# Attention and a capacity-routed mixture of experts on one core: high parts of late w2 pieces ahead of the plane copies, one expert's last roundings 6 matmuls sooner, and a small product kept in PSUM

## The chip, the cores and the metric

The kernel runs on one core of one Trainium2 chip. The metric is device time in microseconds (us), lower is better. The time before is a median of 895.79 us over 3 runs (895.22 to 896.08).

The core's engines run side by side, each through its own list of instructions in order, and they wait for one another by semaphores: TensorE (PE in the profile; PEld is its weight load), VectorE (DVE), ScalarE (ACT), GpSimd (POOL) and SyncE (SP). SBUF is the on-chip working memory; PSUM is the memory that matmuls write and that the other engines, GpSimd excepted, read.

## The reference

Two stages. Attention on 8 x 12 heads, 448 rows of 64, with scores capped by a tanh, gives x of 3584 tokens x 768 features. Then each token goes to exactly one of 8 experts, each of which takes at most 448 tokens, in the order of all (token, expert) logits:

```python
logits = x @ w_gate                       # 3584 x 8
for idx in np.argsort(-logits.flatten()):
    tok, e = idx // E, idx % E
    if assigned[tok] >= 0 or counts[e] >= cap: continue
    assigned[tok] = e; counts[e] += 1
for e in range(E):
    h = np.maximum(x[mask_e] @ w1[e], 0.0)   # 448x768 @ 768x1024
    out[mask_e] = h @ w2[e]                  # 448x1024 @ 1024x768
```

All of it is float32.

## The kernel before

**Three stages.** Attention comes first (to about 330 us of the span). A first choice follows, and from about 381 us to the end the experts run one after the other. Experts are called 0 to 7 here, in the order in which they run; the "third expert" is expert 2. This case is about experts 2 to 6.

**An expert.** Its two products are 144 and 176 matmuls. A float32 operand is split into a high part, rounded to the matmul's faster float32 format, and a low part that is the difference, and a product is the sum high x high, high x low, low x high. In `ffn1` (line 869) eight column blocks of w1 (pieces 0 to 7) are multiplied into the gathered tokens. In `ffn2` (line 900) the work is eight units: units 0 to 3 are the four token tiles with the first half of the output columns (pieces 0 to 3 of w2), units 4 to 7 the same tiles with the second half (pieces 4 to 7). In unit 4 the 16 matmuls with high parts come first, then the 8 with low parts, two for each of pieces 4, 5, 6, 7.

**Splitting weights.** `cut` (lines 757 to 765) makes the two parts of a piece: ScalarE writes the high part (line 760, `w1h` or `w2h`), GpSimd the low part (line 764, `w1l` or `w2l`), which reads both the raw piece and the high part in SBUF. A tiny memset (`gap`, line 762) stands ahead of each on GpSimd. `split1` and `split2` call it for w1 and w2. Where in the order of matmuls a split is recorded is written out by hand: `at` for those during `ffn1`, and, for the late pieces of w2, the line in the loop over u that the change edits.

**The tokens of the next expert.** While an expert is in `ffn2`, the tokens of the next are gathered by four indirect DMAs that GpSimd issues (line 789). ScalarE then splits each tile's words into two planes of 16 bits (`pl`, line 811, "plane copies") and writes them to memory (`xz`), SyncE issues two transposing DMAs that bring them back with features on the partitions (line 815), and `cutt` rounds them into high parts (`xgh`, line 821, ScalarE) and low parts (`xgl`, on GpSimd at line 828 for the first 256 tokens, on VectorE at line 823 for the other 192). These roundings are four entries of a list `bg`, each with a first and a last place, counted in matmuls.

**The choice.** Which tokens the next expert takes is found by a search that runs beside all this: VectorE counts how many candidates lie over each of a few thresholds (line 504, and line 501 on ScalarE), a small matmul sums the counts over the partitions (line 509), VectorE narrows the thresholds (lines 513, 517), and so on for some 12 rounds. `search` ends with three small VectorE instructions on 112 x 8 numbers: a product (line 573), its maximum (575) and the expert that has it (578). `finalise` makes the list of tokens from it. Before a new search, `propose` prepares the candidates in some 20 VectorE instructions (lines 444 to 468), several of which read two tensors in SBUF.

**What sets the order.** PE, ACT, DVE, POOL and SP are scheduled by hand: each engine executes in the order in which the Python code records. `tick` counts the matmuls recorded and lets the other work in at given counts; the choice's rounds are put between the matmuls at fixed distances, so that PE does a round's small matmul at its place in the order whether or not the counts came early.

Of the kernel before, what the change touches and what calls it, by code (L numbers as in the profile page):

```python
# [6 lines left out]
F32=mybir.dt.float32; F32R=mybir.dt.float32r; BF16=mybir.dt.bfloat16; F16=mybir.dt.float16; I32=mybir.dt.int32; I16=mybir.dt.int16  # L7
# [325 lines left out]
class Routing:  # L333
# [189 lines left out]
    def search(s,wp,turned=()):  # L523
        nc=s.nc; v=nc.vector
        post=None
        if turned:
            for h in range(s.NC//16):
                if ("VA",h) not in turned: s.turn("VA",h)
            late=[lambda: s.propose_b(s.NC-4,s.NC,PB(nc)),lambda: None,lambda: s.key(s.NC-4,s.NC)]
            post=lambda: s.flips(s.pm.tile([128,512],F32,name="psM"))  # L530
        else: late,post=s.turns()
        yield 5
        yield from s.select(wp,s.V["VA"],"A",late,post)
        q=s.V["q"][:,:s.NV]
        vb,vc=s.vps[:,:s.NV],s.vps[:,s.NV:2*s.NV]
        if s.cur==0: s.warm(WT)
        v.scalar_tensor_tensor(q,s.V["VA"][:,:s.NV],s.tA,vb,op0=ALU.subtract,op1=ALU.add)
        s.R=[]
        def total(a,b):
            t=wp.tile([128,1],F32,name="tot",bufs=4); jk=wp.tile([128,1],F32,name="jk",bufs=2)  # L540
            v.tensor_scalar(jk,a,b,None,op0=ALU.add,op1=ALU.add,accum_out=t)
            return t
        R=wp.tile([128,16],F32,name="R",bufs=2)
        def row(a,b):
            th=total(a,b)
            r=R[:,len(s.R)*8:len(s.R)*8+8]; jk=wp.tile([128,1],F32,name="jk",bufs=2)
            v.tensor_scalar(r,s.e8,th,None,op0=ALU.mult,op1=ALU.add,accum_out=jk)
            s.R.append(r)
        s.row=lambda th: row(th,s.k8s)
        tA=s.tA; keep=[]  # L550
        yield 4
        yield from s.select(wp,s.V["q"],"B",[lambda: keep.append(total(tA,s.zero))])
        v.scalar_tensor_tensor(q,q,s.tA,vc,op0=ALU.subtract,op1=ALU.add)
        tB=s.tA
        if s.cur==0: s.warm(WT)
        yield 4
        k2=s.vps[:112,448:448+s.NC]
        def copy(): nc.scalar.activation(k2,s.T["K2"],AF.Copy)
        if s.cur<EW:
            mid=[copy,lambda: s.best(wp,0,s.spread(keep[0],tB),k2)]  # L560
            part=[]
            s.row=lambda th: part.append(s.spread(s.k8s,th))
        else: mid=[lambda: row(keep[0],tB),copy]
        yield from s.select(wp,s.V["q"],"C",mid)
        if s.cur>=EW:
            yield 4
            s.pw=s.psum()
            nc.tensor.matmul(s.pw[:112,0:16],s.onesf,R,start=True,stop=True)
            s.best(wp,0,s.pw[:112,0:8],k2); s.pw=s.pw[:112,8:16]
        else:  # L570
            s.pw=part[0]; s.warm(4)
        tt=wp.tile([112,8],F32,name="wt")
        v.tensor_tensor(tt,s.pw,s.wm,op=ALU.mult)
        s.wB=wp.tile([112,1],F32,name="wB")
        v.tensor_reduce(s.wB,tt,axis=AX.X,op=ALU.max)
        s.e8s=wp.tile([112,1],F32,name="e8s")
        sx=wp.tile([112,8],F32,name="sx")
        v.scalar_tensor_tensor(sx,tt,s.wB,s.e8c,op0=ALU.is_equal,op1=ALU.mult,accum_out=s.e8s)
# [108 lines left out]
def ffn_all(nc, tc, ctx, rt, xs, xz, w1, w2, out, ident, E, wp, deferred, xctx, gen):  # L687
# [20 lines left out]
    m=0  # L708
# [48 lines left out]
    def cut(key,r,shape,name,bufs,eng=None,view=lambda t:t,use=lambda t:t):  # L757
        h=ws.tile(shape,F32R,name=name+"h",bufs=bufs)
        l=ws.tile(shape,F32R,name=name+"l",bufs=bufs)
        nc.scalar.activation(view(h),r,AF.Copy)  # L760
        if not eng:
            if tt[0]: nc.gpsimd.memset(gap,0.0)  # L762
            lp[0]=False; tt[0]=True
        (eng or nc.gpsimd).tensor_tensor(view(l),r,view(h).bitcast(F32),op=ALU.subtract)  # L764
        spl[key]=(use(h),use(l))
# [3 lines left out]
    def split2(p,n):  # L769
        hf,i=order(p)[n]  # L770
        view=use=lambda t:t.rearrange("p (o d) -> p o d",o=2)
        cut((p,2,hf,i),raw[p,2,hf,i],[128,2*HD],"w2",8,None,view,use)
# [6 lines left out]
    def newx(p):  # L779
        if p not in xgT: xgT[p]=(fp.tile([128,DC,C],F32R,name="xgh"),fp.tile([128,DC,C],F32R,name="xgl"))  # L780
# [35 lines left out]
    def cutt(p,k,c0,c1):  # L816
        newx(p)
        o,n=((0,256),(256,192))[k]
        h,l=(t[:,c0:c1,o:o+n] for t in xgT[p])
        x=xgp[k][:,c0*n:c1*n].rearrange("p (c t) -> p c t",c=c1-c0)  # L820
        nc.scalar.activation(h,x,AF.Copy)  # L821
        if k:
            nc.vector.tensor_tensor(l,x,h.bitcast(F32),op=ALU.subtract)
            if not lk[0]: cnt[0]-=5
            return
        if tt[0]: nc.gpsimd.memset(gap,0.0)
        lp[0]=False; tt[0]=True
        nc.gpsimd.tensor_tensor(l,x,h.bitcast(F32),op=ALU.subtract)
# [5 lines left out]
    bg=[]  # L834
# [4 lines left out]
    def tick(n=1):  # L839
        cnt[0]+=n; bc[0]+=n; now[0]+=n  # L840
        if bc[0]>=BG:
            if pend: bc[0]=0; scatter(*pend.pop(0))
        if len(res)>cur[0]+1 and cur[0]+1 not in xgs:
            bc[0]=0; n=cur[0]+1; gather(n)
            if n>=FT:
                xq.extend((now[0]+TD+TJ*j,lambda j=j: planes(j)) for j in range(4))
                xq.extend(((n-1)*320+248+8*f,lambda f=f: split1(n,f)) for f in range(2))
                o=(n-1)*320; g=now[0]-o; a=max(262,g+92); b=max(284,g+120)
                bg.extend((o+x,o+min(y,316),z) for x,y,z in ((a,a+18,lambda: cutt(n,0,0,3)),(a,a+34,lambda: cutt(n,0,3,6)),(b,b+(4 if n==FT else 26),lambda: cutt(n,1,0,3)),(b,b+22,lambda: cutt(n,1,3,6))))
        while xq and xq[0][0]<=now[0]: xq.pop(0)[1]()  # L850
        if bg and bg[0][1]<=now[0]: bg.pop(0)[2]()
        if cnt[0]>=hint[0]:
            cnt[0]=0; step()
# [75 lines left out]
    for p in range(E):  # L929
        lastp=p==E-1; cur[0]=p  # L930
        for f in range(FC):
            for n in ((2,3),(4,),(5,),(6,),(7,),(),(),())[f] if p==0 else ((2,),(3,),(4,),(5,),(6,),(7,),(),())[f]: load2(p,n)
            if f+W1B-1<FC and (p==0 or f+W1B-1>=W1B): load1(p,f+W1B-1) if (p,1,f+W1B-1) not in raw else None
            work={}
            if f+2<FC and (p,1,f+2) not in spl: work[3]=[lambda: split1(p,f+2)]
            at={0:{1:[(11,0)],2:[(11,1)],3:[(11,2)],4:[(11,3)],5:[(11,4)],6:[(3,5),(11,6)],7:[(3,7)]},1:{k:[(11,k)] for k in range(FC)},2:{**{k:[(11,k)] for k in range(6)},6:[(8,6)]},E-1:{k:[(11,k)] for k in range(FC)}}.get(p,{k:[(11,k)] for k in range(5)})
            for m,n in at.get(f,()): work[m]=[lambda n=n: split2(p,n)]
            if p==1 and f==0: work[1]=[lambda: xtr(1,4)]; work[4]=[lambda: xtr(1,5)]
            ffn1(p,f,work)
        if lastp:  # L940
            while pend: scatter(*pend.pop(0))
            ih=f2.tile([128,2],I32,name="ih")
            for k in range(2): nc.gpsimd.tensor_scalar(ih[:,k:k+1],res[p][0][:,2:3],2.0,float(k),op0=ALU.mult,op1=ALU.add)
            nc.gpsimd.drain()
            lp[0]=False
            out2=out.rearrange("n (q d) -> (n q) d",q=2)
            for t,hf in [(t,hf) for t in (3,0,1,2) for hf in range(2)]:
                ffn2(p,t,hf,[])
                if t==2: put(out2,ih[:,hf:hf+1],ons[p][0][:,t*DM+hf*HD:t*DM+hf*HD+HD])
                elif hf==1: scatter(p,t)  # L950
            break
        for u in range(8):
            if p+1<FT:
                if u==4: load1(p+1,0); load1(p+1,1)
                if u==5: load1(p+1,2); load2(p+1,0)
            if u==6:
                if p+1>=FT: load1(p+1,2); load2(p+1,0)
                load1(p+1,3)
            if u==7: load2(p+1,1)
            wk={5:{14:[lambda: split1(1,0)]},6:{8:[lambda: split1(1,1)]}}.get(u,{}) if p==0 else {}  # L960
            if p<1 and u==7: wk={15:[lambda: xtr(1,3)]}
            if p>1:
                for m,n in ({3:[(2,7)]} if p==2 else {2:[(14,5),(20,6)],3:[(2,7)]}).get(u,()): wk[m]=wk.get(m,[])+[lambda n=n: split2(p,n)]
            ffn2(p,u%4,u//4,CL[u] if p+1<FT else [],wk)
            if u>3: pend.append((p,u%4))

# [58 lines left out]
```

## Time and profile before

| what | value |
|---|---|
| median of 3 runs | 895.79 us (895.22 to 896.08) |
| the profiled execution, its own time | 895.64 us |
| its span on the core | 893.8 us, granted TensorE clock 1.00 |
| PE busy | 861.8 us, 96% of the span |
| PEld busy | 629.2 us, 70% |
| DVE busy | 595.9 us, 67% |
| ACT busy | 583.9 us, 65% |
| POOL busy | 371.8 us, 42% |
| first matmul of expert 2 | 513.17 us |
| expert 3: first of `ffn2`, first of expert 4 | 607.38 us, 640.22 us |

Times in the profile are counted from the start of the span. A row of the timeline is start, duration, engine, line, operation, the tiles as out<-in, the number of instructions merged into the row, and in square brackets the idle time of the engine just before with what ended it. Matmuls overlap one another, so a wait of PE is best read on PEld, whose weight loads follow one another at the pace of the matmuls: the idle time of PEld before a load, over the usual gap, is time that PE loses.

### The profile page before, as it was taken

The page shows a single profiled execution, that of the slowest core. Times are in us where ns is not written, and L with a number is a line of the kernel's source. Part 1 is how long each engine was busy: PE and PEld are TensorE (multiplying, and loading weights), DVE is VectorE, ACT ScalarE, POOL GpSimd, SP SyncE. Part 2 cuts the span into 40 slices and gives each one's busy share as a digit, 9 for nine tenths or more (in the row PEclk, how much of TensorE's full clock was granted, in tenths as well). Part 3 has the DMA queues.
Part 4 walks back from the last instruction along what each step waited for, and adds up shares of the span by engine and source line. Part 5 has one row for each costly group of instructions (what it writes and reads, how often), then busy time and mean ns, then how long its engine had stood idle before and what let it go on. Part 6 is the DMA issues. An engine that isn't in the chain of part 4 may idle for free.

```text
span 893.8 us, 17555 instructions
## 1 busy us (share of the span) xinstructions
PE 861.8 (96%) x6198; PEld 629.2 (70%) x6198; DVE 595.9 (67%) x2020; ACT 583.9 (65%) x822; POOL 371.8 (42%) x528
## 2 busy tenths in 40 slices
PE   7899999999999997899999999999999999999997
PEld 4334444444333335788989989989889989999997
DVE  3788988989887888767777677777767772130210
ACT  6988898889899957274383683664645735425521
POOL 8100000000000007574585593683864855856941
PEclk9999999999999999999999999999999999999999
DMA  8799999997995007770931874846926927828601
GB/s 121 114 131 144 129 170 171 142 166 105 213 179 85 1 4 250 237 227 1 314 94 51 247 234 128 253 150 195 285 86 186 283 63 211 284 75 250 205 10 54
DMA packets 336121, 139.61 MB, mean 156 GB/s; under 512 B 258304, under 2 KB 325632, under 8 KB 335520
## 3 DMA queue, kind: packets, MB, share of 16 engines
q1 hardware_dynamic: 326448, 107.96, 55.5%
q0 software_dynamic: 4656, 22.02, 7.2%
q10 hardware_dynamic: 4928, 8.49, 2.6%
q8 instruction: 49, 0.80, 0.4%
q14 instruction: 40, 0.33, 0.1%
HBM read 97.15 MB, written 33.03 MB: 146 GB/s over the span
## 4 chain that ended last, share of the span: by engine, by line
PE 70%; issue 12%; DVE 6%; POOL 4%; DMA 3%; SPq 2%; ACT 2%; POOLq 0%; DVEq 0%; ACTq 0%
PE psH L869 23%; PE psH L900 14%; PE psA L189 12%; PE psS L148 10%; PE psM L206 4%; POOL xg L789 2%; PE psS L153 2%; SPq L92 2%; PE psM L37 1%; DVE es L165 1%; POOL w2l L764 1%; POOL out_dram L882 1%; DVE cmpD L504 1%; DMA xg<-xz 1%; DMA k<-in_k_dram 1%
## 5 line engine op out<-in xcount | busy, mean ns | idle before, releaser
L900 PE MATMUL psH<-w2h,hh 128*128 128x384 f32 x896 | 235.2, 340 | 0.0
L900 PE MATMUL psH<-w2l,hh 128*128 128x384 f32 x512 | 167.5, 341 | 3.6 <-POOL gap L762 3.6
L154 ACT ACTIVATE e<-psS 128x896 f32<-128x896 f32 x168 | 147.5, 909 | 30.8 <-PE psS L148 18.0
L900 PEld LDWEIGHTS psH<-w2h,hh 128*128 128x128 f32 x896 | 161.8, 188 | 0.3
L159 ACT ACTIVATE e<-e,bias 128x1792 f32<-128x1792 f32 (+2 forms) x74 | 147.3, 1991 | 2.0
L869 PE MATMUL psH<-xgh,w1h 128*128 128x448 f32 x384 | 143.2, 373 | 1.0 <-ACT xgh L821 0.7
L869 PE MATMUL psH<-xgh,w1l 128*128 128x448 f32 x384 | 141.4, 368 | 0.0
L148 PE MATMUL psS<-tq,tk 64*64 64x448 f32 x1152 | 129.9, 544 | 7.4 <-ACT e L154 4.8
L869 PE MATMUL psH<-xgl,w1h 128*128 128x448 f32 x384 | 136.7, 369 | 0.0
L764 POOL TENSOR_TENSOR w2l<-w2r,w2h 128x768 fp32r<-128x768 f32 x64 | 118.0, 1846 | 42.7 <-ACT w2h L760 42.7
L460 POOL TENSOR_SCALAR r_Bt<-r_b 112x4 f16<-112x4 int32 x1 | 0.2, 201 | 304.1 <-DVE rin L243 304.1
L764 POOL TENSOR_TENSOR w1l<-w1r,w1h 128x768 fp32r<-128x768 f32 x62 | 114.3, 1845 | 19.0 <-ACT w1h L760 14.3
L189 PE MATMUL psA<-e,nv 64*64 64x448 f32 x1104 | 120.5, 540 | 1.2 <-DVE xT L199 1.2
L165 DVE TENSOR_TENSOR es<-es,e 64x896 f32<-64x896 f32 (+2 forms) x74 | 100.3, 1356 | 2.6 <-ACT e L159 1.3
L900 PEld LDWEIGHTS psH<-w2l,hh 128*128 128x128 f32 x512 | 95.5, 188 | 5.7 <-POOL gap L762 5.6
L148 PEld LDWEIGHTS psS<-tq,tk 64*64 64x64 f32 x1152 | 43.7, 132 | 73.2 <-issue 37.9
L875 ACT ACTIVATE hh<-psH 128x448 fp32r<-128x448 f32 x64 | 34.8, 543 | 86.0 <-PE psH L869 79.7
L877 DVE SCALAR_TENSOR_TENSOR hh<-psH,hh 128x64 fp32r<-128x64 f32 (+1 forms) x128 | 43.9, 385 | 67.0 <-ACT hh L875 66.0
L189 PEld LDWEIGHTS psA<-e,nv 64*64 64x64 f32 x1104 | 46.4, 133 | 59.1 <-issue 49.6
L906 ACT ACTIVATE on<-psH 128x384 f32<-128x384 f32 x48 | 23.4, 487 | 90.2 <-PE psH L900 85.9
L869 PEld LDWEIGHTS psH<-xgh,w1h 128*128 128x128 f32 x384 | 72.5, 189 | 6.6 <-ACT xgh L821 1.0
L869 PEld LDWEIGHTS psH<-xgh,w1l 128*128 128x128 f32 x384 | 72.3, 188 | 5.2
(340 smaller groups left out, 1321.5 us busy)
## 6 DMA issues: line engine op xcount, KB each, us to landing
w1r<-in_moe_w_dram SPq DMA_DIRECT2D x64, 384.0 KB, 4.7
w2r<-in_moe_w_dram SPq DMA_DIRECT2D x64, 384.0 KB, 6.8
k<-in_k_dram SPq DMA_DIRECT2D x92, 112.0 KB, 3.4
q<-in_q_dram SPq DMA_DIRECT2D x92, 112.0 KB, 3.9
nv<-in_v_dram SPq DMA_DIRECT2D x72, 128.0 KB, 3.9
xz<-pl ACTq DMA_DIRECT2D x18, 384.0 KB, 3.0
xs<-xn SPq DMA_DIRECT2D x4, 1344.0 KB, 7.0
xs<-xn SPq DMA_DIRECT2D x4, 896.0 KB, 5.2
```

Source lines behind the costliest of these rows:

```text
L148: for c in range(2): nc.tensor.matmul(ps[c*64:c*64+64,h,:S],tks[g,0][hp,o,u*128+c*64:u*128+c*64+64],tks[g,1][hp,o,:],start=True,stop=True)
L154: nc.scalar.activation(ev(g,r),ps[:,:,:S],AF.Tanh,scale=sr[0])
L159: act=lambda: nc.scalar.activation(e,e,AF.Exp,scale=sr[1],bias=bias)
L165: t=es_t[g]; add=lambda o,a,b: nc.vector.tensor_tensor(o,a,b,op=ALU.add)
L189: nc.tensor.matmul(avp[g,o][h*64:h*64+64,:S],lhs,rhs[hp,h,:],start=(j==0 and x==0),stop=j==3)
L206: nc.tensor.matmul(ps[g*32:g*32+32,:S],lhs,rhs,start=first,stop=last)
L764: (eng or nc.gpsimd).tensor_tensor(view(l),r,view(h).bitcast(F32),op=ALU.subtract)
L869: nc.tensor.matmul(ps[:,:C],a[:,c,:],b[:,c,:],start=(m==0),stop=(m==DC*3-1)); m+=1
L875: nc.scalar.activation(h[:,:C],ps[:,:C],AF.Relu)
L877: nc.vector.scalar_tensor_tensor(h[:,d:d+b-a],ps[:,a:b],0.0,h[:,a:b].bitcast(F32),op0=ALU.max,op1=ALU.subtract)
L900: nc.tensor.matmul(ps[:,:HD],h[:,f,a:a+128],spl[p,2,hf,f//2][w][:,f%2,:],start=(m==0),stop=(m==nm-1))
L906: if t<3: nc.scalar.activation(ons[p][0][:,t*DM+hf*HD:t*DM+hf*HD+HD],ps[:,:HD],AF.Copy)
```

## The change

Three edits.

1. In `search`, for all choices but the first, the product of line 573 is written to 8 free columns of the PSUM tile from which its factor comes (`tt=s.pw[:112,16:24]`), and no longer to an SBUF tile `wt`. Lines 575 and 578 read it there.
2. The roundings of the second half of the tokens of expert 2 get earlier places: the 118 in place of 120 moves both by 2 matmuls, and the first is due at once in place of 4 matmuls later, the second 7 in place of 22 matmuls later, though neither later than matmul 316 of the 320 of an expert, before as now. For the other experts the recorded order stays as it was.
3. The late pieces of w2 are split at other places of `ffn2`: for experts 3 to 6 pieces 5, 6 and 7 all in unit 0 (after matmuls 6, 12, 18), no longer in units 2 and 3; for expert 2, piece 7 in unit 1 and no longer in unit 3.

```diff
@@ search
             nc.tensor.matmul(s.pw[:112,0:16],s.onesf,R,start=True,stop=True)
-            s.best(wp,0,s.pw[:112,0:8],k2); s.pw=s.pw[:112,8:16]
+            s.best(wp,0,s.pw[:112,0:8],k2); tt=s.pw[:112,16:24]; s.pw=s.pw[:112,8:16]
         else:
-            s.pw=part[0]; s.warm(4)
-        tt=wp.tile([112,8],F32,name="wt")
+            s.pw=part[0]; s.warm(4); tt=wp.tile([112,8],F32,name="wt")
         v.tensor_tensor(tt,s.pw,s.wm,op=ALU.mult)
@@ tick
-                o=(n-1)*320; g=now[0]-o; a=max(262,g+92); b=max(284,g+120)
-                bg.extend((o+x,o+min(y,316),z) for x,y,z in ((a,a+18,lambda: cutt(n,0,0,3)),(a,a+34,lambda: cutt(n,0,3,6)),(b,b+(4 if n==FT else 26),lambda: cutt(n,1,0,3)),(b,b+22,lambda: cutt(n,1,3,6))))
+                o=(n-1)*320; g=now[0]-o; a=max(262,g+92); b=max(284,g+118)
+                bg.extend((o+x,o+min(y,316),z) for x,y,z in ((a,a+18,lambda: cutt(n,0,0,3)),(a,a+34,lambda: cutt(n,0,3,6)),(b,b+(0 if n==FT else 26),lambda: cutt(n,1,0,3)),(b,b+(7 if n==FT else 22),lambda: cutt(n,1,3,6))))
@@ the loop over u in ffn_all
-                for m,n in ({3:[(2,7)]} if p==2 else {2:[(14,5),(20,6)],3:[(2,7)]}).get(u,()): wk[m]=wk.get(m,[])+[lambda n=n: split2(p,n)]
+                for m,n in ({1:[(2,7)]} if p==2 else {0:[(6,5),(12,6),(18,7)]}).get(u,()): wk[m]=wk.get(m,[])+[lambda n=n: split2(p,n)]
```

The changed kernel has one line fewer, so its lines from 571 on are numbered one lower.

How the order of instructions moves, at two places. First ScalarE in expert 3, from the last block of `ffn1` to the end of unit 3 of `ffn2`, before (`hh` is the result of an `ffn1` block, `on` and `y` that of an `ffn2` unit):

```order
L875 ACTIVATE hh<-psH 128x448 x3
L906 ACTIVATE on<-psH 128x384
L811 ACTIVATE pl<-xg_4110 128x1536
L812 DMA xz_62<-pl 128x1536
L811 ACTIVATE pl<-xg_4110 128x1536
L812 DMA xz_62<-pl 128x1536
L811 ACTIVATE pl<-xg_4111 128x1536
L812 DMA xz_63<-pl 128x1536
L906 ACTIVATE on<-psH 128x384
L811 ACTIVATE pl<-xg_4111 64x1536
L812 DMA xz_63<-pl 64x1536
L760 ACTIVATE w2h<-w2r 128x768 x2
```

The same place in the changed kernel:

```order
L874 ACTIVATE hh<-psH 128x448 x3
L759 ACTIVATE w2h<-w2r 128x768 x3
L905 ACTIVATE on<-psH 128x384
L810 ACTIVATE pl<-xg_4110 128x1536
L811 DMA xz_62<-pl 128x1536
L810 ACTIVATE pl<-xg_4110 128x1536
L811 DMA xz_62<-pl 128x1536
L810 ACTIVATE pl<-xg_4111 128x1536
L811 DMA xz_63<-pl 128x1536
L905 ACTIVATE on<-psH 128x384
L810 ACTIVATE pl<-xg_4111 64x1536
L811 DMA xz_63<-pl 64x1536
```

All three high parts have moved from behind the four plane copies to a place ahead of the first, and ahead of the first `on`. The lists of PE, SP and POOL are the same as before, instruction for instruction: on GpSimd the low parts of pieces 5, 6 and 7 stand right behind the four gathers, before and now.

Second, ScalarE at the end of expert 1, where the tokens of expert 2 are rounded, before:

```order
L821 ACTIVATE xgh<-xg_4110 128x3x256
L906 ACTIVATE on<-psH 128x384
L821 ACTIVATE xgh<-xg_4111 128x3x192 x2
```

and now:

```order
L820 ACTIVATE xgh<-xg_4110 128x3x256
L820 ACTIVATE xgh<-xg_4111 128x3x192
L905 ACTIVATE on<-psH 128x384
L820 ACTIVATE xgh<-xg_4111 128x3x192
```

The first rounding of the second half has moved ahead of the result of unit 6. VectorE's list is the same as before in its order at all places.

## The prediction

> **What bounds the kernel now.** I read the page's busy times first, then the list of waits, then the timeline of PEld around each of its waits behind line 900, and last ACT, POOL and DVE in the same stretches.
>
> ```profile
> PE 861.8 (96%) x6198; PEld 629.2 (70%) x6198; DVE 595.9 (67%) x2020; ACT 583.9 (65%) x822; POOL 371.8 (42%) x528
> POOL w2l L764 <- ACT w2h L760: 42.7, 9, 8.3
> PEld psH L900 <- POOL gap L762: 5.6, 7, 1.5
> ```
>
> TensorE is the bound: it is busy for 96% of the span, so an edit is worth the PE idle time that it removes, no more. The two other rows are from the list of waits (total us, times, longest us). PE's weight loads in `ffn2` wait 5.6 us in all for GpSimd, in 7 waits. GpSimd, which makes the low parts, waits 42.7 us for high parts of w2. The 7 waits stand in the timeline of PEld:
>
> ```profile
> 564.51 0.30 PEld L900 LDWEIGHTS psH<-w2l,hh 128*128 128x128 f32 x2 [0.23 <-POOL gap L762]
> 628.10 0.30 PEld L900 LDWEIGHTS psH<-w2l,hh 128*128 128x128 f32 x2 [0.86 <-POOL gap L762]
> 691.58 0.19 PEld L900 LDWEIGHTS psH<-w2l,hh 128*128 128x128 f32 x1 [0.77 <-POOL gap L762]
> 753.98 0.30 PEld L900 LDWEIGHTS psH<-w2l,hh 128*128 128x128 f32 x2 [0.54 <-POOL gap L762]
> 755.78 0.30 PEld L900 LDWEIGHTS psH<-w2l,hh 128*128 128x128 f32 x2 [1.50 <-POOL gap L762]
> 816.00 0.30 PEld L900 LDWEIGHTS psH<-w2l,hh 128*128 128x128 f32 x2 [0.16 <-POOL gap L762]
> 817.79 0.30 PEld L900 LDWEIGHTS psH<-w2l,hh 128*128 128x128 f32 x2 [1.50 <-POOL gap L762]
> ```
>
> They lie in experts 2 (0.23), 3 (0.86), 4 (0.77), 5 (2.04) and 6 (1.66), all in unit 4, where the low parts of the late pieces are first read: 5.56 us. Why they are late, in expert 3:
>
> ```profile
> 607.57 0.55 ACT L875 ACTIVATE hh<-psH 128x448 fp32r<-128x448 f32 x1 [3.53 <-PE psH L869]
> 611.87 0.49 ACT L906 ACTIVATE on<-psH 128x384 f32<-128x384 f32 x1 [3.75 <-PE psH L900]
> 613.43 1.49 ACT L811 ACTIVATE pl<-xg 128x1536 int16<-128x1536 int16 x1 [1.07 <-DMA xg<-xs,idx]
> 621.59 1.58 ACT L760 ACTIVATE w2h<-w2r 128x768 fp32r<-128x768 f32 x2 [0.57 <-ACT pl L811]
> ...
> 614.70 0.09 POOL L762 MEMSET gap<- 1x1 f32 x1
> 622.51 1.86 POOL L764 TENSOR_TENSOR w2l<-w2r,w2h 128x768 fp32r<-128x768 f32 x1 [7.72 <-ACT w2h L760]
> 626.20 1.84 POOL L764 TENSOR_TENSOR w2l<-w2r,w2h 128x768 fp32r<-128x768 f32 x1
> ```
>
> ACT makes the high parts only after the plane copies, which wait for the gather. POOL, done with its gathers at 614.70, idles 7.72 us, then needs three times 1.84 us and ends at 628.04. PE goes on at 628.10.
>
> **Edit 3, part by part.** Moved are three ACT instructions in each of experts 3 to 6 and one in expert 2. Between `hh` (ends 608.12) and `on` (starts 611.87) ACT idles 3.75 us; three high parts take 2.4 (1.58 for two, 0.8 each). They fit, and no plane copy, transpose or load moves. If that cover were gone, each 0.8 would delay the gathered tokens' planes, whose rounding in expert 2 was waited for by PE (below). POOL can then start at 614.79, end at 620.3 and wait for nothing that PE needs; 628.04 - 620.3 = 7.7 us earlier, against 0.86 lost. In experts 5 and 6 the same move covers 2.04 and 1.66. So all seven waits go: **-5.6 us**. GpSimd's next work, the low parts of w1, waits for high parts that ACT still makes after the plane copies, so it gains little, and is not late either.
>
> What is late next? The search's next small matmul after the wait:
>
> ```profile
> 626.47 0.44 DVE L504 TENSOR_SCALAR_CACHE_REDUCE cmpD<-r_VAt,r_H8A 128x224 bf16<-128x224 f16 x1
> 628.73 0.18 PE L509 MATMUL psR<-r_cd,r_bo 128*128 128x4 bf16 x1
> ```
>
> Its counts are ready at 626.9 and PE comes at 628.73; 0.86 sooner it still comes 0.9 after them. Each round starts anew from PE's matmul, so the gain stays.
>
> **Edit 3, the price.** GpSimd now works from 614.79 to 620.3, where it idled, and VectorE is then at the end of `propose`:
>
> ```profile
> 614.61 0.42 DVE L463 TENSOR_TENSOR r_VC<-r_P,r_Ct 112x256 f16<-112x256 f16 x1
> 614.94 0.18 DVE L464 TENSOR_TENSOR r_K<-r_At,r_Bt 112x32 f32<-112x32 f16 x1
> 615.04 0.18 DVE L468 SCALAR_TENSOR_TENSOR r_K<-r_kk,r_Ct 112x32 f32<-112x32 f16 x1
> 615.98 0.39 DVE L483 CAST r_VAt<-psR 128x224 f16<-128x224 f32 x1 [0.75 <-PE psR L478]
> 617.14 0.44 DVE L504 TENSOR_SCALAR_CACHE_REDUCE cmpD<-r_VAt,r_T8A 128x224 bf16<-128x224 f16 x1
> 618.47 0.18 PE L509 MATMUL psR<-r_cd,r_bo 128*128 128x4 bf16 x1
> ...
> 678.26 0.09 POOL L762 MEMSET gap<- 1x1 f32 x1
> 679.21 0.39 DVE L483 CAST r_VAt<-psR 128x224 f16<-128x224 f32 x1 [0.41 <-PE psR L478]
> ...
> L578 DVE SCALAR_TENSOR_TENSOR sx<-wt,wB,r_e8c x7: 227/228/5410, 363.7 to 722.2; 112x8 f32<-112x8 f32 x7
> 659.19 0.34 DVE L578 SCALAR_TENSOR_TENSOR sx<-wt,wB,r_e8c 112x8 f32<-112x8 f32 x1
> 722.21 5.41 DVE L578 SCALAR_TENSOR_TENSOR sx<-wt,wB,r_e8c 112x8 f32<-112x8 f32 x1
> 725.76 1.84 POOL L764 TENSOR_TENSOR w1l<-w1r,w1h 128x768 fp32r<-128x768 f32 x1
> ```
>
> Lines 463, 464 and 468 read two SBUF tensors each. So does line 578 (its row of all seven gives least, median and most in ns), and it shows what that can cost: a 0.23 us instruction took 5.41 and ended at 727.62, when the last of three GpSimd subtractions ended (727.60); in the choice at 659.19 it lost only 0.11. In the changed kernel line 463 runs when the first w2l comes (614.79), and 464 and 468 stand right behind it. If VectorE keeps its turn for these last 0.28 us, GpSimd starts 0.4 us late and nothing is lost: lower bound 0. If 464 and 468 lose one subtraction (1.85), line 483 comes 1.0 us later, and the counts, 0.89 us ahead of PE's matmul at 618.47, cost it 0.1; in expert 4, where line 483 comes 0.95 us after the gap and not 1.28, 0.4. Two subtractions cost 1.9 and 2.3, three 3.8 and 4.1. Experts 2, 5 and 6 are spared: in 2 there is one w2l only, and in 5 and 6 no search follows that would wait for these instructions. So the price is 0 to 7.9 us. I take **0**, since the three VectorE instructions overlap at their ends (464 starts 0.09 before 463 ends), so that GpSimd finds no gap between them.
>
> The Trainium skill ("SBUF — State Buffer", Who interferes with whom) states that VectorE with two SBUF inputs and a reading GpSimd instruction contend for one port pair, that whichever issues first holds it for the whole instruction, and that the other blocks. The 5.41 us row agrees as to the blocking, but not that it lasts one instruction. By issue order alone the w2l of 614.79 would come before line 464 of 614.94, and the second w2l before line 468.
>
> **Edit 1.** With the product in PSUM line 578 reads one SBUF tensor, and the 5.41 us row should not come again. The PE wait behind it, and a reduction of the size of line 575's that reads PSUM:
>
> ```profile
> 729.12 0.36 PE L869 MATMUL psH<-xgl,w1h 128*128 128x448 f32 x1
> 729.66 0.16 PE L618 MATMUL psR<-scan,r_lo 112*112 112x2 f16 x1 [0.18 <-DVE ei L612]
> 729.74 0.45 PE L869 MATMUL psH<-xgh,w1l 128*128 128x448 f32 x1
> ...
> L588 DVE TENSOR_REDUCE wA<-psR x7: 154/166/168, 357.9 to 721.3; 112x1 f32<-112x8 f32 x7
> ```
>
> PE idles 0.18 us for `finalise`'s matmul, and two successive `ffn1` matmuls stand 0.62 us apart where 0.20 is the pace; so between 0.18 and 0.42, of which the two small matmuls between them need some: **-0.3 us**. The rest of the 5.2 us hid behind a list that is not due until then. The other five choices wait nowhere on PE for it. Reading PSUM makes a reduction no longer than 0.17 us; VectorE writing 8 columns to PSUM is shown nowhere. Hundredths more or less cost nothing, since these instructions stand well ahead of the matmul that waits.
>
> **Edit 2.** The rounding that moves ahead of `on` waits for the transpose anyway:
>
> ```profile
> 510.31 0.47 ACT L906 ACTIVATE on<-psH 128x384 f32<-128x384 f32 x1
> 512.43 1.26 ACT L821 ACTIVATE xgh<-xg 128x576 fp32r<-128x576 f32 x2 [1.65 <-DMA xg<-xz]
> 513.16 0.19 PEld L869 LDWEIGHTS psH<-xgh,w1h 128*128 128x128 f32 x1 [1.04 <-ACT xgh L821]
> 513.82 0.75 DVE L823 TENSOR_TENSOR xgl<-xg,xgh 128x576 fp32r<-128x576 f32 x1
> 517.27 0.18 PE L509 MATMUL psR<-r_ce,r_bo 128*128 128x8 bf16 x1
> ```
>
> ACT had finished `on` and idled 1.65 us until the DMA landed at 512.41, so the 1.04 us that PE loses stay. Now `on` falls between the two roundings, the second comes 0.35 us later, and with it the low part on DVE (513.82), behind which the search's next round waits. PE took that round's matmul at 517.27 with no time to spare. Between 0 and 0.45 us lost: **+0.2**.
>
> **The sum.** -5.6 - 0.3 + 0.2 = -5.7 on the profiled execution's 895.64 us gives 889.9; the median of the runs lies 0.15 above it: **890.0 us**.
>
> **The rivals.** (a) *Turns.* GpSimd takes the port between 463 and 464 and again between 464 and 468, two subtractions in experts 3 and 4: -5.7 + 1.9 + 2.3 = -1.5, 894.3 us. For it speaks the row at 659.19, where the waiting engine got in after one instruction; against it that 464 is already under way. By the Trainium skill's rule of issue order this is what comes. (b) *Starved.* VectorE waits out all three, as at 722.21: -5.7 + 3.8 + 4.1 = +2.2, 898.0, slower. It decides from a third subtraction on, in both experts. Against it: it was seen once in two meetings of this kind. (c) *The search takes over* as bound in experts 2 to 4, and the 1.9 us there are lost: 891.9. The 0.9 us to spare at 628.73 speak against it. (d) *It doesn't do what it says*: POOL waits for something else than the high parts, say the landing of the gathers, and starts as late as before: 895.7. Against it: in the list of waits ACT w2h ends the idle time, and the raw pieces were loaded in `ffn1`.
>
> **How the numbers follow.** Forecast 0.55, (a) 0.17, (b) 0.08, (c) 0.10, (d) 0.10. The forecast's own range is 889.2 (all bounds at their good end, and 0.4 of spread) to 891.0 (0.5 for one subtraction lost in both, 0.25 more in edit 2). With (c) and (a) the range is 889.2 to 894.4, which leaves out (b), (d) and a little. About 0.2%, 1.8 us, is what a measurement of this kernel can tell from no change. Faster: the forecast, (c) and half of (a), which lies near that limit, 0.74; same: (d) and the other half, 0.18; slower: (b), 0.08.
>
> **What would show it.** Right: no PEld wait behind `gap` in units 4 of experts 3 to 6, w2l starting right after the fourth gather, plane copies where they were. Line 578 at 0.23 us in every choice after the first. The wait at the start of expert 2 still about 1 us, and some tenths at the second small matmul after it. Wrong: lines 464 or 468 of some microseconds, a PE wait at the first small matmul of the search in experts 3 and 4, or w2l that start late for another reason.

## The result: slower by 0.8%

| | before | changed |
|---|---|---|
| median, measured side by side | 896.12 us (895.22 to 899.36, 6 runs) | 903.06 us (901.73 to 906.09, 6 runs) |
| ratio changed / before | | 1.0078, 95% interval 1.0057 to 1.0100 |
| profiled execution, its own time | 895.64 us | 901.73 us |
| its span, mean granted clock | 893.8 us, 1.000 | 899.9 us, 0.996 |

The forecast was 890.0 us, with 889.2 to 894.4 as its range. The time lies far above it, beyond the slower rival's 898.0 too.

The length of each stage, from its first weight load to the first of the next, shows where the time went (changed minus before, us; stages of the experts that are not shown differ by less than 0.1):

| stage | forecast | measured |
|---|---|---|
| expert 1 `ffn2`, with the wait that opens expert 2 | 0 | -0.67 |
| expert 2 `ffn1` (edit 2) | +0.2 | +0.33 |
| expert 2 `ffn2` | -0.23 | -0.15 |
| expert 3 `ffn2` | -0.86 | **+4.97** |
| expert 4 `ffn2` | -0.77 | **+5.40** |
| expert 5 `ffn1` (edit 1) | -0.3 | -0.34 |
| expert 5 `ffn2` | -2.04 | -1.99 |
| expert 6 `ffn2` | -1.66 | -1.56 |

So the gains came, and experts 3 and 4 lost them again twice over. Lines from 571 on are numbered one lower here than in the kernel before. First a row of the list of waits (total us, times, longest us), in the kernel before and in the changed one, and then two groups of the changed kernel's page (busy us, mean ns of one, idle us ahead of them and what ended it):

```profile
PE psR L509 <- DVE cmpD L504: 5.4, 13, 0.7
PE psR L509 <- DVE cmpD L504: 14.2, 16, 4.4
```

```profile
L899 PE MATMUL psH<-w2l,hh 128*128 128x384 f32 x512 | 167.2, 342 | 0.0
L763 POOL TENSOR_TENSOR w2l<-w2r,w2h 128x768 fp32r<-128x768 f32 x64 | 118.0, 1845 | 2.9 <-ACT w2h L759 2.8
```

Nothing in `ffn2` waits for low parts any more, and GpSimd waits for high parts of w2 for 2.8 us in all, no longer 42.7. In their place PE waits for counts of the search. The timeline in expert 3: line 461 in the kernel before, and behind the dots the changed kernel, VectorE and then GpSimd:

```profile
614.14 0.17 DVE L461 TENSOR_SCALAR r_Ct<-r_c 112x32 f16<-112x32 int32 x1
...
613.67 0.18 DVE L460 TENSOR_SCALAR r_Bt<-r_b 112x32 f16<-112x32 int32 x1
613.76 6.13 DVE L461 TENSOR_SCALAR r_Ct<-r_c 112x32 f16<-112x32 int32 x1
619.81 0.41 DVE L462 TENSOR_TENSOR r_VB<-r_P,r_Bt 112x256 f16<-112x256 f16 x1
620.58 0.18 DVE L468 SCALAR_TENSOR_TENSOR r_K<-r_kk,r_Ct 112x32 f32<-112x32 f16 x1
...
614.37 1.85 POOL L763 TENSOR_TENSOR w2l<-w2r,w2h 128x768 fp32r<-128x768 f32 x1
616.20 1.86 POOL L763 TENSOR_TENSOR w2l<-w2r,w2h 128x768 fp32r<-128x768 f32 x1
618.04 1.80 POOL L763 TENSOR_TENSOR w2l<-w2r,w2h 128x768 fp32r<-128x768 f32 x1
```

Line 461, an instruction of 0.17 us, takes 6.13. It ends at 619.89, when the third subtraction does (619.84), and starts 0.6 us before the first is recorded. The rest of `propose` follows at its usual pace, some 5.9 us late. What PE makes of it:

```profile
622.34 0.16 PE L509 MATMUL psR<-r_cd,r_bo 128*128 128x4 bf16 x1 [4.09 <-DVE cmpD L504]
625.21 0.52 PE L899 MATMUL psH<-w2l,hh 128*128 128x384 f32 x1
625.53 0.52 PE L899 MATMUL psH<-w2h,hh 128*128 128x384 f32 x1
625.85 0.52 PE L899 MATMUL psH<-w2l,hh 128*128 128x384 f32 x1
626.17 0.42 PE L899 MATMUL psH<-w2h,hh 128*128 128x384 f32 x1
626.44 0.34 PE L899 MATMUL psH<-w2l,hh 128*128 128x384 f32 x1
626.61 0.34 PE L899 MATMUL psH<-w2h,hh 128*128 128x384 f32 x1
626.79 0.34 PE L899 MATMUL psH<-w2l,hh 128*128 128x384 f32 x1
```

PE stands still for 4.09 us, and a second loss follows that no part of the prediction had: about ten matmuls start 0.32 us apart in place of 0.17 (625.21, 625.53, 625.85, 626.17), and then the pace is back (626.44, 626.61, 626.79). That is ten times 0.15, 1.5 us more. Two stretches of the changed kernel, of 3.41 us each, show which clock was granted (busy us of PE, PEld, DVE, ACT, POOL with counts, then the clock, the DMA share and GB/s):

```profile
619.54:622.95 3.41, 0.61 (x7) 0.61 (x7) 3.08 (x17) 1.03 (x1) 0.38 (x2) 1.00 0.95 238
622.95:626.36 3.41, 3.41 (x13) 3.41 (x12) 2.59 (x16) 0.49 (x1) 0.00 (x0) 0.50 0.46 126
```

The stall and the low clock together are the stage's loss: 4.97 + 0.81 = 5.78 us against the kernel that keeps the gain of 0.81 (below), of which 4.09 are the wait and 1.69 what came behind it. Expert 4 repeats it: line 461 from 682.30 for 6.12 us, a wait of 4.42 us, some ten slow matmuls.

The theory to be tried has two parts. GpSimd's three subtractions, back to back, keep VectorE out of what both need until the last one ends; and after PE has stood still for some 4 us its clock is low for a while. The rivals: the moved instructions on ScalarE, or edits 1 and 2, made the search late; VectorE loses single turns only; the clock fell for another reason.

### The profile page after: what moved, and what is told of

Same layout as the page of the kernel before. It is cut to its first block, busy times and chain, and to the rows that moved or that the text cites. A ratio compares the mean times of both kernels' runs of the same rounds, so it can differ in the third digit from the quotient of the medians.

```text
span 899.9 us, 17551 instructions
## 1 busy us (share of the span) xinstructions
PE 862.8 (96%) x6198; PEld 631.8 (70%) x6198; DVE 610.5 (68%) x2020; ACT 583.5 (65%) x822; POOL 371.5 (41%) x528
## 4 chain that ended last, share of the span: by engine, by line
PE 81%; DVE 8%; issue 3%; DMA 3%; SPq 3%; ACT 2%; POOL 0%; POOLq 0%; DVEq 0%; ACTq 0%
PE psH L868 26%; PE psH L899 21%; PE psA L189 12%; PE psS L148 10%; PE psM L206 4%; SPq L92 2%; PE psS L153 2%; DVE r_Ct L461 1%; DVE cmpD L504 1%; PE psM L37 1%; DVE es L165 1%; DMA xg<-xz 1%; PE psL L37 1%; DMA k<-in_k_dram 1%; DMA xg<-xs,idx 1%
## 5 line engine op out<-in xcount | busy, mean ns | idle before, releaser
L899 PEld LDWEIGHTS psH<-w2h,hh 128*128 128x128 f32 x896 | 163.7, 191 | 0.1
```

The costliest lines, as they stand in the source:

```text
L899: nc.tensor.matmul(ps[:,:HD],h[:,f,a:a+128],spl[p,2,hf,f//2][w][:,f%2,:],start=(m==0),stop=(m==nm-1))
```

## The experiments

Single executions differ by several us outside the edited places (24 runs of the kernel before, beside the first four experiments, gave 894.78 to 904.16 us, median 896.76). In the profiles that comes mostly from the wait that opens expert 2, where the transposing DMA lands sooner or later; the stage in front of it differs from that of the kernel before by -0.75 to +2.77 us. So stages are compared below, and times are given with their intervals.

### Each edit without the others

Edit 3 undone, edits 1 and 2 kept:

```diff
-                for m,n in ({1:[(2,7)]} if p==2 else {0:[(6,5),(12,6),(18,7)]}).get(u,()): ...
+                for m,n in ({3:[(2,7)]} if p==2 else {2:[(14,5),(20,6)],3:[(2,7)]}).get(u,()): ...
```

> The changed kernel with edit 3 undone; edits 1 and 2 stay. Theory (the loss is GpSimd's three subtractions back to back, which hold up the end of propose on VectorE in experts 3 and 4): line 461 takes 0.2 us again, no wait of PE over 0.6 us at the first small matmul of the search, granted clock 1.00, the seven waits of PEld behind gap are back; 0.3 us less than before by edit 1 and between 0.4 less and 0.3 more by edit 2, so 895.0 to 895.8 us in the profiled execution. Rival (edits 1 or 2 shift the search so that it comes late): PE still waits about 4 us in experts 3 and 4, and the time stays near 902 us.

Measured: 897.29 us (12 runs), ratio 0.9997 (0.9974 to 1.0019). `ffn2` of experts 3 and 4 is 0.09 and 0.06 us longer than before, line 461 takes 0.18 us, the clock is 1.000. Expert 5's `ffn1` gains 0.33. The profiled execution took 898.46 us, above the range expected, and 2.32 us of that is the DMA that opens expert 2. The kernel before with edit 3 alone, the same two lines the other way round:

> The kernel before with edit 3 alone. Theory: both waits of about 4 us of PE and the slow matmuls behind them are there as in the changed kernel, line 461 takes about 6 us in experts 3, 4 and 5; 902 to 903 us, since only the 0.3 us of edit 1 and some tenths of edit 2 are missing. Rival (it takes edits 1 or 2 as well): no such waits, 890 to 891 us.

Measured: 905.6 us, ratio 1.0094 (1.0067 to 1.0122); `ffn2` of experts 3 and 4 +4.84 and +5.21, line 461 at 6.15 us in both, PE waits of 4.11 and 4.44 us (in expert 5 the line held up was 454, not 461, for 5.94 us). The loss is edit 3's alone. The excess of some 3 us over the expectation is, in the profiled execution (906.91 us), again the DMA at expert 2: 2.77 us in the stage ahead of it, and 1.42 in the one behind, with a lesson of its own, told below at the clock.

### Where the early place costs, and where not

Edit 3 in experts 2, 5 and 6 only:

```diff
-  ({1:[(2,7)]} if p==2 else {0:[(6,5),(12,6),(18,7)]})
+  ({1:[(2,7)]} if p==2 else {2:[(14,5),(20,6)],3:[(2,7)]} if p<5 else {0:[(6,5),(12,6),(18,7)]})
```

> The changed kernel with edit 3 in experts 2, 5 and 6 alone; in experts 3 and 4 the high parts stay behind the plane copies. Theory: no wait of about 4 us anywhere, because in 5 and 6 no search follows propose, although line 461 still takes about 6 us in expert 5; the gains of experts 2, 5 and 6 remain (0.23 + 2.04 + 1.66) with the 0.3 of edit 1: 4.2 us less than before, 891.0 to 891.9 us. Rival (early high parts cost something in every expert, through ScalarE's order): the gain is smaller than 2 us, 893.5 us or more.

Measured: 893.54 us (12 runs), ratio 0.9973 (0.9954 to 0.9993). Experts 5 and 6 gain 1.99 and 1.56, as in the changed kernel, while expert 5's row still reads

```profile
742.93 6.17 DVE L461 TENSOR_SCALAR r_Ct<-r_c 112x32 f16<-112x32 int32 x1
```

The same hold-up costs nothing where no search follows. The time is 1.6 us above the expected range: the waits behind `gap` in experts 3 and 4, which stay in this kernel, were 1.13 and 1.50 us for 0.86 and 0.77 before, the DMA came 0.25 later, and edit 2 cost 0.48 in this profile, where the expectation had let it gain.

### The early place without the meeting

All of the change, but the low parts of the early pieces are recorded a few matmuls later (GpSimd's order stays the same), and ahead of the first of them, in experts 2, 3 and 4, GpSimd copies a number that line 468 writes:

```diff
-            if tt[0]: nc.gpsimd.memset(gap,0.0)
+            if first_early_piece: nc.gpsimd.tensor_copy(gap,rt.T["K2"][0:1,0:1])
+            elif tt[0]: nc.gpsimd.memset(gap,0.0)
```

> The whole change, but in experts 2, 3 and 4 GpSimd's memset of gap ahead of the first early subtraction is replaced by a copy of one number that line 468 writes, so that GpSimd starts only when propose is done. ScalarE's order is that of the changed kernel. Theory: propose ends at its old pace (line 461 0.2 us), the subtractions start about 0.3 us behind line 468, end about 1 us later than in the changed kernel and still 6 us before PE needs them; no wait behind gap, no wait at the search, granted clock 1.00: 5.6 + 0.3 us less than before and some tenths by edit 2, 889.2 to 890.0 us. Rival (the loss comes from ScalarE's new order): the waits of 4 us stay, about 902 us. Rival (VectorE is held up in the search too): a wait of 1 to 4 us moves to the next small matmul of the search, 893 to 900 us.

Measured: 891.00 us (7 runs), ratio 0.9955 (0.9924 to 0.9986); the profiled execution 890.75. Its timeline in expert 3:

```profile
614.76 0.18 DVE L461 TENSOR_SCALAR r_Ct<-r_c 112x32 f16<-112x32 int32 x1
615.66 0.18 DVE L468 SCALAR_TENSOR_TENSOR r_K<-r_kk,r_Ct 112x32 f32<-112x32 f16 x1
...
615.98 0.18 POOL L762 COPY gap<-r_K 1x1 f32<-1x1 f32 x1 [0.66 <-DVE r_K L468]
616.13 1.83 POOL L765 TENSOR_TENSOR w2l<-w2r,w2h 128x768 fp32r<-128x768 f32 x1
```

The profiled execution is 0.75 us above the expected range; the time before the experts was 0.7 us longer in it, and edit 2 cost 0.34. GpSimd waits 0.66 us, VectorE not at all. No wait behind `gap` is left, and PE's longest wait for the counts is 0.7 us. The terms are now to be seen alone: -0.33, -0.81, -0.72, -1.99 and -1.56 us in `ffn2` of experts 2 to 6, together -5.4. ScalarE's order is that of the changed kernel, so it is not the cause. Against this kernel the hold-up cost the changed one 4.97 + 0.81 = 5.8 us in expert 3 and 5.40 + 0.72 = 6.1 in expert 4.

### Does VectorE keep its turn?

The prediction took the price as 0 because lines 462 to 468 overlap at their ends. To put that to the test GpSimd waits for line 461 (it copies a number of `Ct`, not of `K2`), in experts 3 and 4; so the subtractions come while lines 463 and 464 are at work.

> The whole change, but in experts 3 and 4 GpSimd's first early subtraction waits (by a copy of one number in place of the memset of gap) for line 461 and no longer, so that lines 462, 463, 464 and 468, which read two SBUF tensors each, are still to come when the three subtractions begin. Theory (GpSimd leaves VectorE no turn until the last of three subtractions ends): one of these four lines takes 5 to 6 us in both experts, PE waits 4 to 5 us at the search's first small matmul, the clock falls behind it; 901 to 904 us. The prediction's reason (the four lines overlap, so VectorE keeps its turn until line 468 is done): no such row, 889 to 891 us. Turns (one subtraction each time): one or two of the lines take about 1.9 us, PE loses 0.4 to 2 us in each of the two experts, 890.5 to 894 us.

Measured: 903.22 us, ratio 1.0052 (1.0021 to 1.0084). Expert 3, and then expert 4:

```profile
615.25 6.00 DVE L463 TENSOR_TENSOR r_VC<-r_P,r_Ct 112x256 f16<-112x256 f16 x1
621.17 0.18 DVE L464 TENSOR_TENSOR r_K<-r_At,r_Bt 112x32 f32<-112x32 f16 x1
684.89 5.62 DVE L464 TENSOR_TENSOR r_K<-r_At,r_Bt 112x32 f32<-112x32 f16 x1
...
615.49 1.84 POOL L765 TENSOR_TENSOR w2l<-w2r,w2h 128x768 fp32r<-128x768 f32 x1
619.17 1.79 POOL L765 TENSOR_TENSOR w2l<-w2r,w2h 128x768 fp32r<-128x768 f32 x1
688.66 1.79 POOL L765 TENSOR_TENSOR w2l<-w2r,w2h 128x768 fp32r<-128x768 f32 x1
```

Line 463 starts 0.24 us before the first subtraction and ends with the third (620.96), at 621.25; line 464 starts 0.10 before and ends at 690.51, the third at 690.45. Being under way saves neither. The stages lose 5.71 and 5.63 us. The waits of PE, 3.77 and 3.99 us, are a little under the 4 to 5 expected, but the clock stays at 0.50 for 6.83 us, twice as long as in the changed kernel, so that 2.75 and 2.36 us are lost behind them (5.71 + 0.81 - 3.77, 5.63 + 0.72 - 3.99). This refutes the reason on which the price of 0 stood.

The other side of it: the second of the three subtractions waits for line 468, the first comes as early as in the changed kernel.

> The whole change, but in experts 3 and 4 the second of GpSimd's three early subtractions waits for line 468 (by a copy of one number in place of the memset of gap); the first comes as early as in the changed kernel. Theory: line 461 is held up by the first subtraction alone, about 2.5 us as in expert 2 of the changed kernel, and goes on when it ends; PE loses 0.4 to 1.2 us in each of the two experts, no fall of the clock; 890 to 892 us. If the length of the hold-up doesn't come from subtractions that follow one another, line 461 still takes about 6 us and the time stays near 902 us.

Measured: 893.01 us (9 runs), ratio 0.9947 (0.9925 to 0.9970). In expert 3:

```profile
616.74 2.51 DVE L461 TENSOR_SCALAR r_Ct<-r_c 112x32 f16<-112x32 int32 x1
617.34 1.85 POOL L765 TENSOR_TENSOR w2l<-w2r,w2h 128x768 fp32r<-128x768 f32 x1
620.24 0.18 POOL L762 COPY gap<-r_K 1x1 f32<-1x1 f32 x1 [1.05 <-DVE r_K L468]
```

Line 461 is let go when the one subtraction ends (619.19), takes 2.51 us and not 6.13, and the waits of PE are 0.47 and 0.83 us. So the length of the hold-up is that of the row of subtractions without a pause. (The time is 1 us above the expected range; the DMA at expert 2 came 1.6 us later in this profile.)

### Is it GpSimd's reading?

In experts 3 and 4 each early subtraction is replaced by two memsets of the same tile, so that GpSimd writes and reads nothing (the low parts of these pieces are left out); in the second kernel it also waits for line 461 first.

```diff
-            nc.gpsimd.tensor_tensor(view(l),r,view(h).bitcast(F32),op=ALU.subtract)
+            for _ in range(2): nc.gpsimd.memset(l.bitcast(F32),0.0)
```

> The changed kernel, but in experts 3 and 4 each of GpSimd's three early subtractions is replaced by two memsets of the same low part, so that GpSimd works at that place but reads nothing (the low parts of these pieces are left out: they are zero). If what holds VectorE up is GpSimd's reading of SBUF, line 461 takes 0.2 us in experts 3 and 4 and nothing waits there, as in the kernel that waits for line 468: 889 to 891 us. If any work of GpSimd that follows work holds it up, line 461 (which reads one tensor) still takes until the last memset ends, some microseconds, and PE waits at the search.

> The same memsets in place of the subtractions of experts 3 and 4 (low parts left out again), and GpSimd waits for line 461 first, so that lines 462 to 468, with two tensors in SBUF each, meet them. If the second tensor's read port is what is fought for, lines 463 and 464 take 0.4 and 0.2 us, where they took 6.0 and 5.6 us against the subtractions, and there is no wait of PE: 889 to 891 us. If any work of GpSimd will do, one of them is held up until the last memset ends.

Measured, one execution each: 890.72 and 891.75 us, and `ffn2` of experts 3 and 4 at -0.81 and -0.72 us in both, as with the wait for line 468. (The second lies 0.75 us above its expected range; the time before the experts was 1.0 us longer in it, and the DMA at expert 2 came 0.5 us later.) The first kernel in expert 3, and after the dots the second:

```profile
614.63 1.48 DVE L460 TENSOR_SCALAR r_Bt<-r_b 112x32 f16<-112x32 int32 x1
614.72 1.41 DVE L461 TENSOR_SCALAR r_Ct<-r_c 112x32 f16<-112x32 int32 x1
616.14 0.43 DVE L462 TENSOR_TENSOR r_VB<-r_P,r_Bt 112x256 f16<-112x256 f16 x1
616.48 0.42 DVE L463 TENSOR_TENSOR r_VC<-r_P,r_Ct 112x256 f16<-112x256 f16 x1
615.30 1.57 POOL L767 MEMSET w2l<- 128x768 f32 x2
616.83 1.55 POOL L767 MEMSET w2l<- 128x768 f32 x2
...
616.67 0.18 DVE L468 SCALAR_TENSOR_TENSOR r_K<-r_kk,r_Ct 112x32 f32<-112x32 f16 x1
616.64 1.53 POOL L767 MEMSET w2l<- 128x768 f32 x2
```

The two expectations had one answer each for all of VectorE's lines; the answer is split. Lines 462, 463 and 468, with two SBUF tensors each, run at full speed beside memsets. Lines 460 and 461, with one, are held up even by memsets, but only by about one: 1.48 and 1.41 us, to 616.11 and 616.13, near the end of the first of the pair. So both kinds of VectorE instruction can meet GpSimd, each in its own way, and only the row of subtractions kept VectorE out for all its length. That it is their reading which does it is the likely difference, but not shown alone: a memset is also another instruction, and a shorter one (0.8 us against 1.84).

The Trainium skill ("SBUF — State Buffer", Who interferes with whom) has this division: a VectorE instruction with two SBUF inputs contends only with a GpSimd operation that reads SBUF, and one like line 461 (`tensor_scalar`) can enter a mode that takes the shared ports whatever GpSimd does. The traces agree with both halves in what they time (0.18 to 0.43 us beside memsets, and 1.41), though they don't show which mode line 461 ran in. The prediction used the first half only, and so named lines 463, 464 and 468 and overlooked 461. Of the Trainium skill's rule in the same section that whoever issues first holds the ports for its one instruction and the other waits that long, the traces bear out less: line 461 was recorded 0.6 us ahead of the subtraction and lost, and then it lost three in a row.

### The clock, without GpSimd

The kernel before, with line 463 executed again 12, 17 and 13 more times in experts 2, 3 and 4, so that the search is late while GpSimd idles:

```diff
-        v.tensor_tensor(w("VC"),w("P"),bc(w("Ct")),op=ALU.mult)
+        for _ in range(1+{4:12,5:17,6:13}.get(s.cur,0)): v.tensor_tensor(w("VC"),w("P"),bc(w("Ct")),op=ALU.mult)
```

> The kernel before with line 463 executed again 12, 17 and 13 more times (it writes the same values) in the propose of experts 2, 3 and 4, about 0.34 us each, so that the search comes late with GpSimd idle. The stall of PE at its first small matmul should be about 2.4, 4.1 and 3.0 us. Theory (the granted clock falls because PE has stood still too long, not because of GpSimd's work): slow matmuls and a clock under 1.00 behind the stall of expert 3, as in the changed kernel, about 1.4 us more; behind 2.4 us none, and behind 3.0 us open; 9.5 to 12 us more than before in all, 905 to 908 us. Rival (the fall belongs to the three subtractions or to the changed order): clock 1.00 behind all three stalls.

Measured: 915.22 us, one execution; stalls of 3.26, 7.61 and 4.51 us. They are longer than meant because a repeat takes 0.46 us, not 0.34, and the repeats of expert 3 ran into GpSimd's late subtractions. Expert 2, up to the stall's end and behind it:

```profile
555.00:562.00 7.00, 4.28 (x26) 3.90 (x25) 6.55 (x19) 5.26 (x5) 0.00 (x1) 1.00 0.66 240
562.00:570.00 8.00, 7.46 (x38) 7.30 (x38) 5.49 (x35) 2.80 (x4) 5.52 (x5) 0.79 0.82 180
```

GpSimd is busy for 0.00 us, and yet the clock behind the stall is 0.79. It falls behind all three stalls: the fall belongs to PE's standing still. The kernel with edit 3 alone had it in a place that nobody edited, behind a long wait for the DMA at expert 2. Here are that wait of PEld, the stretch of 3.41 us in which most of it lies and the next one, and a stretch of the same profile early in attention with the next one; behind the dots, the two stretches over which the same wait spreads in the kernel with edit 3 undone:

```profile
516.74 0.19 PEld L869 LDWEIGHTS psH<-xgh,w1h 128*128 128x128 f32 x1 [3.80 <-ACT xgh L821]
514.65:518.06 3.41, 1.32 (x7) 1.07 (x8) 1.34 (x2) 1.95 (x4) 0.00 (x0) 1.00 1.00 325
518.06:521.47 3.41, 3.41 (x11) 3.06 (x10) 2.70 (x16) 2.58 (x6) 2.58 (x3) 0.50 1.09 361
16.31:19.72 3.41, 1.14 (x16) 0.42 (x12) 1.98 (x2) 3.08 (x3) 2.04 (x7) 1.00 0.73 113
19.72:23.13 3.41, 3.41 (x24) 1.63 (x20) 1.20 (x2) 2.80 (x4) 0.00 (x0) 0.50 0.73 117
...
510.50:513.91 3.41, 2.07 (x12) 1.75 (x11) 0.06 (x2) 0.04 (x1) 1.85 (x1) 1.00 0.92 249
513.91:517.33 3.42, 1.72 (x9) 1.43 (x10) 1.49 (x3) 2.42 (x5) 1.09 (x2) 1.00 1.12 334
```

One length of a stall doesn't sort the cases. By PE's own idle time, 3.48 us in the kernel with edit 3 alone brought a fall, and 3.04 us with edit 3 undone brought none. But early in attention the clock fell in seven of the twelve profiles, where no idle time of PE was longer than 2.27 us. What sorts them is the idle time within fixed stretches. Apart from the kernel's end the clock is low for 3.41 or 6.83 us, and within a profile the falls lie whole multiples of 3.41 us apart (622.95 and 691.22 in the changed kernel: 20 times 3.413). In the stretch just ahead of each fall PE was idle for 1.80 us or more, and in no other stretch at full clock for more than 1.89 (counted in steps of 3.41 us back from the last fall of each profile). The 3.48 us put 2.09 us of idle time into one stretch; the 3.04 us were divided, 1.34 and 1.70. So it matters where a stall lies, and not only how long it is. This is read from the twelve profiles afterwards; no run was made to test it.

The Trainium skill ("TensorE: Matmul & The Clock Gate", What's actually happening) states that the clock halves after an idle window of about 3.4 us, counted in windows that run freely. The traces agree on the half (0.50, with a pace of 0.32 us for 0.17) and on windows of 3.41 us that run freely, but PE need not be idle for the whole of one: 1.80 us of it were enough.

### The best of it

The kernel that waits for line 468, with edit 2 undone as well:

> The kernel in which GpSimd waits for line 468, with edit 2 undone. If edit 2 costs what the second small matmul of expert 2 showed (0.3 to 0.5 us of ffn1 there), this stage is 0.3 to 0.5 us shorter, 30.5 to 30.7 us, and the time 0.3 us below that of the kernel with edit 2, 890.5 us. If edit 2 is worth something at the start of expert 2, the wait of PEld for xgh there, counted from the landing of the transposing DMA, is longer, and the time is the same or worse.

Measured: 890.62 us (889.62 to 891.15, 6 runs), ratio 0.9916 (0.9896 to 0.9936), with 888.8 us of span in the profiled execution. `ffn1` of expert 2 takes 30.62 us, as before the change, against 30.95 to 31.10 with edit 2. The first weight load of expert 2 stood 0.75 us behind the landing of the DMA before the change and 0.76 in the changed kernel (landings at 512.41 and 511.84), so edit 2 buys nothing there; its second rounding on ScalarE comes 0.4 us later and with it the low part on VectorE. This version is faster than the kernel before and the changed one.

## Why the prediction was wrong

**Edit 3, what it removes: right.** -5.56 was forecast, -5.4 measured in the kernel that waits for line 468 (experts 2 to 6: 0.33 for 0.23, 0.81 for 0.86, 0.72 for 0.77, 1.99 for 2.04, 1.56 for 1.66). The high parts fitted into ScalarE's 3.75 us, nothing was late behind them, and the search did not take over as bound. Expert 2, called spared, was not quite: line 461 lost one subtraction there too (2.51 us), and the gain was 0.15 in place of 0.33.

**Edit 3, the price: this is the step that failed.** "I take 0, since the three VectorE instructions overlap at their ends, so that GpSimd finds no gap between them." The waits for lines 461 and 468 showed the contrary: lines 463 and 464 lost 6.0 and 5.6 us although under way. What came is the rival called Starved, at 0.08. Its evidence, the 5.41 us of line 578, stood in the trace with just this shape (three subtractions without a pause, an end with the last of them); the row at 659.19 set against it, 0.34 us, was a meeting of another kind. There line 578 began 1.51 us into one subtraction and was let go when it ended, at 659.53, although the next began at 659.50:

```profile
657.68 1.82 POOL L764 TENSOR_TENSOR w1l<-w1r,w1h 128x768 fp32r<-128x768 f32 x1
659.50 1.84 POOL L764 TENSOR_TENSOR w2l<-w2r,w2h 128x768 fp32r<-128x768 f32 x1
```

At 722.21 it began 0.13 us into a subtraction and was held through that one and the two behind it. Edit 3 put the beginning of a subtraction beside VectorE's lines, as at 722.21. Two parts of the step were incomplete besides:
- It looked for victims among lines with two SBUF tensors. The victim was line 461, with one, and 0.6 us ahead of GpSimd's first recorded instant.
- It priced three lost subtractions at 3.8 and 4.1 us, the wait of PE. The waits were 4.09 and 4.42, so 0.6 more in all; the low clock behind them, 1.5 to 1.7 us each time and in no rival, is most of the rest of the 11.9 us that the two experts lost against the price of 7.9.

**Edit 1: right in size.** -0.3 forecast; -0.31 to -0.34 measured in expert 5's `ffn1`, in every kernel that has it. Line 577 (578 before) is no longer held up:

```profile
L577 DVE SCALAR_TENSOR_TENSOR sx<-psR,wB,r_e8c 112x8 f32<-112x8 f32 x6 | 1.4, 226 | 0.2
```

**Edit 2: right in sign, small in size.** +0.2 forecast, inside 0 to 0.45; 0.33 measured in the changed kernel, at the second small matmul of expert 2, as worked out (0.48 in two other profiles, just beyond the bound).

**The range** reached 894.4 because Starved was left out of it. With line 578 at 722.21 as the one meeting of those two that came at the beginning of a subtraction, the bound of 7.9 us ought to have been the likelier end.

## What to carry to other kernels

Before work is moved into an idle stretch of GpSimd, look at what VectorE does in that stretch, one-tensor `tensor_scalar` lines included, and who waits for it: several reading operations of GpSimd without a pause can cost VectorE all of their length. A short wait of GpSimd for VectorE's last such line (0.66 us here) took that cost away and kept the whole gain. And a wait of PE should be priced with what the clock takes behind it, here 1.5 to 2.8 us wherever PE had been idle for more than half of one of the 3.41 us stretches.

## What the hardware showed that was not expected

- One VectorE instruction was held through three GpSimd subtractions (5.4 to 6.2 us), in every profile in which it started between 0.6 us before and 0.13 us after the first subtraction on which it met them, and through one (2.5 us) where only one came. One that started later in a subtraction was let go when that one ended, although the next followed at once: line 578 at 659.19 and in two other profiles (1.51 to 1.55 us after the start), and, in the kernel with the repeated line 463, line 464 (0.26 us after it):

```profile
627.88 1.80 DVE L464 TENSOR_TENSOR r_K<-r_At,r_Bt 112x32 f32<-112x32 f16 x1
627.62 2.00 POOL L764 TENSOR_TENSOR w2l<-w2r,w2h 128x768 fp32r<-128x768 f32 x1 [7.72 <-ACT w2h L760]
629.62 1.83 POOL L764 TENSOR_TENSOR w2l<-w2r,w2h 128x768 fp32r<-128x768 f32 x1
```

So the place of the start sorts every case behind 381 us. Why it decides is open; no run here was made to tell it.
- Line 461 was caught 0.6 us before the recorded start of GpSimd's first subtraction, with the last gather still running; line 460, 0.70 us before it, was not. That GpSimd takes hold of the next operation's data ahead of its recorded start is a guess; the runs only show that without a subtraction in the queue the same line, at the same place behind the gather, takes 0.18 us.
- The granted clock fell to 0.50 behind a fixed stretch of 3.41 us in which PE had been idle for about 1.8 us or more, from whatever cause it waited; a stall of 3.04 us that lay across two stretches (1.34 and 1.70) went free. It stayed low for 3.41 us, some ten matmuls at half pace, and for 6.83 where PE was idle again for 1.05 us or more of the first 3.41.
